# A scan and an MLP in one kernel: the MLP's first product as one run per group of half-height matmuls, with loads on two queues and a new order

## The chip, the cores and the metric

The kernel runs on one core of one Trainium2 chip. The metric is the device time of one execution in microseconds (us). Differences of about 0.2% are what a measurement of this kernel can tell apart. The core has five engines with an instruction stream each: TensorE (PE, matrix products), VectorE (DVE), ScalarE (ACT), GpSimd (POOL) and SyncE (SP, which mostly issues DMA transfers). They run beside each other and wait for each other by semaphores.

## What is computed

The input x is 2048 tokens by D = 448. It is normalised once (xn); from xn come a linear recurrence over the tokens with complex state (448 states, the "scan") and an MLP with F = 1792 hidden units and a layer norm of its own.

```python
xn = _layernorm(x)
# branch s: a diagonal recurrence over the tokens
Lam_bar = jnp.exp(dt * Lam)
Bu = jnp.einsum("bld,pd->blp", xn + 0j, ((Lam_bar - 1.0) / Lam)[:, None] * Bmat)
for t in range(L):
    h = Lam_bar[None, :] * h + Bu[:, t, :]
...
s = 2.0 * jnp.einsum("blp,dp->bld", hseq, Cmat).real + xn * Dskip
# branch g: layer norm, 448 -> 1792, gelu, 1792 -> 448, silu
y = _layernorm(xn)
g = _silu(jnp.einsum("bsf,fd->bsd", _gelu(jnp.einsum("bsd,df->bsf", y, w1) + b1), w2) + b2)
return x + s * g
```

Inputs and output are bf16.

## The kernel before, in words

**Tiling.** The 2048 tokens are 4 groups of 2 blocks of 256 tokens; in a block, even and odd tokens (`par` 0 and 1) lie apart, so that the scan takes 256 steps of two tokens per group. A group goes through these stages:

- layer norm: `ln_stats` (L356-363, DVE), `ln_scale` (L390-415), `ln_apply` (L417-429) writes the scan's input `xn_sb` and the MLP's input `xn2_sb`; `xt` (L431-446) transposes them into `xnT` and `xn2T`, by a DMA on SP, or for group 0's MLP input on PE with a copy by DVE (L446).
- `bu` (L611-624): the scan's input projection, PE at L616, 49 matmuls of 256 columns, in four parts through PSUM bank 4, each copied to `u_sb` by ACT.
- `ssm` (L629-675): the scan. DVE rotates the inputs by the tables WT into `v_sb`, does 7 scans (L641), ACT copies them to `s_b`, and DVE rotates back into `h_sb` (L669-673). Small POOL steps carry the state to the next group.
- `mm1` (L679-693): the MLP's first product. For each of the 7 pairs of F tiles, PE does 8 matmuls (L686) of 128 rows by 128 columns by 512 tokens: 2 F tiles times 4 slices of D. 448 is 3.5 times 128, so the fourth slice holds 64 rows of w1, one row with the bias b1 (against a column of ones in `xn2_sb`), and zeros. One gelu of 1024 columns (ACT, L692) takes both tiles out of PSUM; two pairs of banks take turns. For group 0 `mm1_half` (L695-709) does the same for each half of the tokens, with matmuls of 256 columns (L701), so that it can start on the first 256 tokens.
- `mm2` (L711-721): the second product, 14 matmuls of 448 columns (L715) for each of four quarters of the group, then `o` (DVE, L718), tanh (ACT, L719) and `g_sb` (DVE, L720).
- `skip` (L723-732): the term xn * Dskip for the odd tokens, on POOL or DVE.
- `ym` (L736-774): the output. 7 matmuls (L747) of `h_sb` with CZ (even tokens, with 4 more of the input with M0, L750) or CQ (odd tokens), times `g_sb` (DVE, L756), plus x (DVE, L759), and the transfer out.

Once for all groups, before that: the parameters (L455-530, mostly POOL), the tables WT (`tables`, L536-557, by ACT's Sin), the scaled and transposed B (`lb` L574, `bt`), C loaded (`ldc`, into `Cn`, L250, which is the second half of `gT`'s buffer 1) and transposed into `Cr` by DMA, CQ and CZ (`cq`, by `combine` L560-571: `tmp` on ACT or DVE at L567, then L569 on DVE), and M0 (`m0`, L599-609: four products of CQ with B, PE at L605, each of which needs all seven CQ tiles).

**What sets the order.** Every step above records tasks in a `Plan` with what they read and write. `emit` (L106-137) then goes through a list of task numbers, `ORDER` (L146-164), and gives each engine its instructions in that order; it adds a semaphore wait where a task depends on one of another engine. `SECOND` (L165-167) lists the tasks that run on their second choice of engine. An engine's stream is thus fixed: when its next instruction waits, all behind it wait. Nearly all loads are issued by SP in the order of the list.

```python
        for t in order:
...
            for sem, val in need.items():
                if seen.get(sem, 0) < val:
                    eng.wait_ge(self.sems[sem], val)
```

**PE's order before.** Group 0's first product in halves, its second products (14 + 42 matmuls, with a projection and the whole first product of group 1 in between), then M0, projections, and single pairs of group 2's first product between the other stages, so that each pair of L686 stands among scan and output work.

## Time and profile before

| | |
|---|---|
| runs | 159.75, 159.76, 159.87 us (median 159.76) |
| span of the profiled execution | 159.2 us |
| PE | 946 matmuls, 151.3 us busy (95%) |
| DVE | 265 instructions, 136.9 us (86%) |
| ACT | 151 instructions, 93.2 us (59%) |
| POOL | 51.5 us (32%) |
| TensorE clock granted | full, in all stretches but the last |
| moved by DMA | 14.70 MB, 92 GB/s on average |

The span is the profiler's, from the first to the last instruction of one execution; it is 0.56 us less than the median of the runs. "Busy" counts the time in which an engine has an instruction under way. The chain is the work that ended last, followed backwards from the end to whatever released each step. In lists of instructions a line shows the start, the length, the engine, the line of the kernel, the operation, what it writes and reads, and in brackets the idle time of the engine before it and who ended it. The groups that the steps of the first product make up are these (busy time, mean of one, then idle time of the engine before them and its cause):

```profile
L686 PE MATMUL psum<-xn2T,w_sb 128*128 128x512 bf16 x168 | 38.2, 379 | 0.1
...
L692 ACT ACTIVATE gT<-psum 128x1024 bf16<-128x1024 f32 x21 | 21.4, 1021 | 11.7 <-PE psum L686 11.6
...
L701 PE MATMUL psum<-xn2T,w_sb 128*128 128x256 bf16 x112 | 12.9, 273 | 2.0 <-DMA w_sb<-in_B_w_dram 1.8
```

Matmuls overlap in the array, so one takes 379 ns while the next follows after some 217 ns (1.73 us for eight).

### The profile page before, as it was taken

What the parts mean: (1) busy time and instruction counts of PE and PEld (TensorE: products, weight loads), DVE (VectorE), ACT (ScalarE), POOL (GpSimd) and SP (SyncE); (2) the same over time, 40 slices, a digit from 0 to 9 for tenths busy, and PEclk for the clock granted to TensorE, in tenths of its full rate; (3) what the DMA queues carried; (4) which work ended last, traced back from release to release, by engine and by line L of the source; (5) the groups of instructions that cost most, each with busy time, mean ns of one, the idle gap of its engine ahead of it and who ended that gap; (6) DMA issues with size and microseconds to landing.
All of it is one profiled execution on the core that took longest, in us unless ns stands there. A gap on an engine that the chain in (4) does not pass through costs nothing.

```text
span 159.2 us, 2725 instructions
## 1 busy us (share of the span) xinstructions
PE 151.3 (95%) x946; PEld 93.7 (59%) x946; DVE 136.9 (86%) x265; ACT 93.2 (59%) x151; POOL 51.5 (32%) x127
## 2 busy tenths in 40 slices
PE   6959999999999999999999999999989999999990
PEld 6849965565565556566655555576556655555560
DVE  5478969999998799999789999893999599999982
ACT  3839899997779962689835472212456972450200
POOL 5578840007616000038600573302015420060021
PEclk9999999999999999999999999999999999999998
DMA  4999999888980057000210430213401000010032
GB/s 103 260 303 364 315 149 198 139 161 159 276 172 4 0 100 147 0 0 4 48 20 0 120 65 1 57 21 94 116 4 58 0 4 0 0 58 0 0 115 60
DMA packets 31174, 14.70 MB, mean 92 GB/s; under 512 B 24693, under 2 KB 30713, under 8 KB 31162
## 3 DMA queue, kind: packets, MB, share of 16 engines
q1 hardware_dynamic: 30914, 14.26, 39.4%
q0 software_dynamic: 96, 0.23, 0.4%
q8 instruction: 7, 0.11, 0.3%
q10 hardware_dynamic: 152, 0.05, 0.1%
q14 instruction: 5, 0.04, 0.1%
HBM read 6.89 MB, written 1.84 MB: 55 GB/s over the span
## 4 chain that ended last, share of the span: by engine, by line
PE 88%; DMA 7%; SPq 2%; DVE 1%; issue 0%
PE psum L715 27%; PE psum L686 21%; PE psum L616 13%; PE psum L747 12%; PE psum L701 7%; PE psum L750 4%; DMA w_sb<-in_B_w_dram 4%; PE psum L605 3%; DMA xnT<-xn_sb 3%; SPq L84 2%; PE psum L753 1%; PE psum L440 0%; DVE t L756 0%; DVE tmp L759 0%; PE psum L607 0%
## 5 line engine op out<-in xcount | busy, mean ns | idle before, releaser
L715 PE MATMUL psum<-w_sb,gT 128*128 128x448 bf16 x224 | 43.8, 352 | 0.0
L686 PE MATMUL psum<-xn2T,w_sb 128*128 128x512 bf16 x168 | 38.2, 379 | 0.1
L715 PEld LDWEIGHTS psum<-w_sb,gT 128*128 128x128 bf16 x224 | 21.9, 98 | 20.0
L692 ACT ACTIVATE gT<-psum 128x1024 bf16<-128x1024 f32 x21 | 21.4, 1021 | 11.7 <-PE psum L686 11.6
L686 PEld LDWEIGHTS psum<-xn2T,w_sb 128*128 128x128 bf16 x168 | 18.5, 112 | 15.8 <-issue 0.7
L616 PE MATMUL psum<-xnT,BT 128*128 128x256 bf16 x196 | 24.0, 273 | 0.5 <-DMA xnT<-xn_sb 0.5
L616 PEld LDWEIGHTS psum<-xnT,BT 128*128 128x128 bf16 x196 | 19.0, 98 | 5.8 <-DMA xnT<-xn_sb 1.0
L719 ACT ACTIVATE th<-o 128x448 f32<-128x448 f32 x16 | 9.1, 573 | 16.4 <-DVE o L718 16.3
L641 DVE TENSOR_TENSOR_SCAN s_f<-cw,cur,v_sb 128x256 f32<-128x256 f32 x21 | 15.6, 784 | 0.2
L701 PE MATMUL psum<-xn2T,w_sb 128*128 128x256 bf16 x112 | 12.9, 273 | 2.0 <-DMA w_sb<-in_B_w_dram 1.8
L701 PEld LDWEIGHTS psum<-xn2T,w_sb 128*128 128x128 bf16 x112 | 11.8, 112 | 2.8 <-DMA w_sb<-in_B_w_dram 2.0
L620 ACT ACTIVATE u_sb<-psum 128x512 bf16<-128x512 f32 x12 | 7.2, 596 | 10.2 <-PE psum L616 10.0
L731 POOL TENSOR_TENSOR xd<-xn_sb,dbc 128x448 bf16<-128x448 bf16 x4 | 4.8, 1198 | 24.9 <-DVE dbc L339 13.9
L747 PE MATMUL psum<-CZ,h_sb 128*128 128x448 bf16 x56 | 11.9, 352 | 0.0
L756 DVE TENSOR_TENSOR t<-psum,g_sb 128x448 bf16<-128x448 f32 (+2 forms) x17 | 9.9, 589 | 1.7 <-PE psum L750 1.1
L358 DVE BATCH_NORM_STATS2 lnst<-x_all 128x6 f32<-128x448 bf16 x14 | 8.2, 611 | 3.5 <-DMA x_all<-in_A_x_dram 3.5
L720 DVE SCALAR_TENSOR_TENSOR g_sb<-th,o 128x448 bf16<-128x448 f32 x16 | 10.4, 664 | 0.7 <-ACT th L719 0.6
L718 DVE TENSOR_TENSOR o<-psum,b2bc 128x448 f32<-128x448 f32 x16 | 9.7, 614 | 1.3 <-PE psum L715 1.3
L747 PE MATMUL psum<-CQ,h_sb 128*128 128x448 bf16 (+2 forms) x54 | 10.5, 332 | 0.0
L731 POOL TENSOR_TENSOR xr<-xd,g_sb 128x448 f32<-128x448 bf16 x5 | 5.5, 1106 | 14.6 <-DVE tmp L759 14.5
L707 ACT ACTIVATE gT<-psum 128x512 bf16<-128x512 f32 x14 | 8.3, 590 | 3.2 <-PE psum L701 2.9
L731 POOL TENSOR_TENSOR xr<-x_all,xr 128x448 f32<-128x448 bf16 x6 | 6.9, 1156 | 9.2 <-DVE xr L732 9.1
(157 smaller groups left out, 224.8 us busy)
## 6 DMA issues: line engine op xcount, KB each, us to landing
out_dram<-tmp SPq DMA_DIRECT2D x7, 224.0 KB, 2.0
w_sb<-in_B_w_dram SPq DMA_DIRECT2D x3, 448.0 KB, 7.0
x_all<-in_A_x_dram SPq DMA_DIRECT2D x3, 448.0 KB, 4.4
w_sb<-in_B_w_dram SPq DMA_DIRECT2D x3, 384.0 KB, 6.2
gT<-in_A_C_re_dram SPq DMA_DIRECT2D x1, 392.0 KB, 11.6
Bn<-in_A_B_re_dram SPq DMA_DIRECT2D x1, 336.0 KB, 6.5
Bn<-in_A_B_im_dram SPq DMA_DIRECT2D x1, 336.0 KB, 6.4
gT<-in_A_C_im_dram SPq DMA_DIRECT2D x1, 336.0 KB, 12.0
```

Of the source, the lines that this page charges most:

```text
L616: fns = [lambda e, r=r, m=m, d=d: e.matmul(psum[:, 4, r * NK:(r + 1) * NK], BT[:, m, d, :], xnT[:, gx, d, :], start=(d == 0), stop=(d == 6 ...
L641: dve(lambda e, i=i, ri=ri, init=init: e.tensor_tensor_scan(s_f[:, i, ri, :], col(R2, i).to_broadcast([128, NK]), v_sb[:, i, ri, :], init, ...
L686: fns = [lambda e, k=k, d=d: e.matmul(psum[:, b0 + k, :], w1_sb[:, d, fcol(2 * j + k)], rhs[:, d, :, :], start=(d == 0), stop=(d == 3)) fo ...
L692: act(lambda e: e.activation(gT[:, gb, 2 * j:2 * j + 2, :], psum[:, b0:b0 + 2, :], ACT.Gelu_apprx_tanh), [f"ps{b0}", f"ps{b0 + 1}"] + (WK ...
L701: fns = [lambda e, k=k, d=d: e.matmul(psum[:, banks[k], :].rearrange("p (r c) -> p r c", r=2)[:, :, cs], w1_sb[:, d, fcol(2 * j + k)], rhs ...
L715: fns = [lambda e, fi=fi: e.matmul(psum[:, bk, 0:D], gT[:, gb, fi, q * 128:(q + 1) * 128], w2_sb[:, fi, :], start=(fi == 0), stop=(fi == N ...
L718: dve(lambda e: e.tensor_tensor(o2[:, fb, :], psum[:, bk, 0:D], b2bc[:], ALU.add), [f"ps{bk}", "b2bc"], [f"oo{fb}"], 0.62, prio - 76)
L719: act(lambda e: e.activation(th[:, fb, :], o2[:, fb, :], ACT.Tanh, scale=0.5), [f"oo{fb}"] + (WK + WKP if g == 0 else []), [f"th{fb}"], 0. ...
L720: dve(lambda e: e.scalar_tensor_tensor(out=g_sb[:, gs, :], in0=th[:, fb, :], scalar=1.0, in1=o2[:, fb, :], op0=ALU.add, op1=ALU.mult), [f" ...
L731: kb.either(("pool", lambda e, o=o, i0=i0, i1=i1, op=op: e.tensor_tensor(o, i0, i1, op), 1.37, 0.15), ("dve", lambda e, o=o, i0=i0, i1=i1, ...
L747: fns = [lambda e, k=k: e.matmul(psum[:, bk, c0:c1], h_sb[:, hb, k, k0:k0 + 128], cm[:, k, c0:c1], start=(k == 0), stop=False) for k in ra ...
L756: dve(lambda e: e.tensor_tensor(t3[:, fb, c0:c1], psum[:, bk, c0:c1], g_sb[:, gs, c0:c1], ALU.mult), [f"ps{bk}", f"g{gs}"], [f"t3{fb}_{c0} ...
```

## The change

- `mm1` and `mm1_half` become `mm1_run`. It does a whole group (or a token half of group 0) in one run. Each matmul uses 64 rows of the array instead of 128: the upper and lower half of the rows work on different F tiles of a pair. In phase one, F tile 0 takes its upper 64 rows of three slices and F tile 1 its lower 64; in phase two they swap, with a fourth matmul each for the half slice. So a pair is 6 + 8 = 14 half-height matmuls. Pair j + 1's phase one is issued before pair j's phase two.
- There are three pairs of PSUM banks for it (four in group 0's run), `MB`. The bias is no longer a row of w1 but an operand of the gelu (`b1f`); a pair has two gelus of 512 (or 256) columns for one of 1024 (or 512).
- The 64 last rows of w1 are loaded into rows 64 to 127 of slice 3, and 64 rows of slice 2 are copied to rows 0 to 63 of slice 3 (`w1c`, 4 copies, two on DVE and two on ACT). `xn2_sb` repeats 64 columns to match (`tcols`), so `ln_apply` for the MLP is two instructions for groups 1 to 3. The memsets of the padding go.
- C is staged in the scan's tiles `vs` (`v_sb` and `s_b` together) instead of in `gT`.
- Loads may be issued by ACT instead of SP; some are.
- Group 0's layer norm scales are worked out for both blocks together on DVE; group 1's chain of small steps moves to POOL. `skip` is split in two parts.
- `ORDER` and `SECOND` are new. The stages are recorded in the order of `STEPS`. PE's order after: group 0's run in halves; three of its second products; pairs of group 1's run (whole), with projections of group 0 and the fourth second product towards its end; then the first M0 product, with projections and second products between the four of them; group 2's run; two second products; the first output; one pair of group 3's run; the other outputs of groups 0 and 1, with group 2's projections and other second products between them; the rest of group 3's run, and then its remaining stages.

Instructions: PE 946 to 1156, DVE 265 to 260, ACT 156 to 195, POOL 129 to 138, as the programs list them.

```diff
-            def mm1(g, j, prio):
...
-            def mm1_half(j, b, k3, prio):
...
+            MB = ((0, 1), (2, 3), (4, 7), (5, 6))
+
+            def mm1_run(g, b, n0, prio):
+
+                gx = gb = g % 2
+                cols = slice(0, 256) if b is None else slice(b * 128, (b + 1) * 128)
+                rhs = xn2T[:, gx, :, cols].rearrange("p (r d) c -> p d r c", r=2)
...
+                def phase(j, second):
+
+                    c = chunk[2 * j]
+                    bk = MB[j % 3 if g else (n0 + j) % 4]
+
+                    def one(k, n, h):
+                        rows, d = slice(64 * h, 64 * h + 64), (0, 1, 2 + h, 3 - h)[n]
+                        return lambda e: e.matmul(view(bk[k]), w1_sb[rows, d, fcol(2 * j + k)], rhs[rows, d, :, :], start=not second and n == 0, stop=second and n == 3)
+                    pe([one(h if not second else 1 - h, n, h) for n in range(4 if second else 3) for h in (0, 1)],
+                       xk2 + [f"w1_{c}", f"w1r_{c}"] + ([f"w1c_{c}"] if second else []), [f"ps{bk[0]}", f"ps{bk[1]}"], prio=prio)
+                    if second:
+                        act([lambda e, k=k: e.activation(gT[:, gb, 2 * j + k, :].rearrange("p (r c) -> p r c", r=2)[:, :, cols], view(bk[k]), ACT.Gelu_apprx_tanh,
+                                                         bias=b1f[:, 2 * j + k:2 * j + k + 1]) for k in range(2)],
...
+                for j in range(8):
+                    if j < 7:
+                        phase(j, False)
+                    if j:
+                        phase(j - 1, True)
...
-                ld("sp", w1_sb[0:64, 3, a:a + w], dram_ap(B_w1, 384 * F + a, [[F, 64], [1, w]]), [f"w1r_{c}"], 64 * w * 2, prio)
+                ld("sp", w1_sb[64:128, 3, a:a + w], dram_ap(B_w1, 384 * F + a, [[F, 64], [1, w]]), [f"w1r_{c}"], 64 * w * 2, prio)
+                low, high = w1_sb[0:64, 3, a:a + w], w1_sb[64:128, 2, a:a + w]
+                kb.either(("dve", lambda e: e.tensor_copy(low, high)), ("act", lambda e: e.activation(low, high, ACT.Copy)), [f"w1_{c}"], [f"w1c_{c}"])
...
-        Cn = gT[:, 1, 6:14, :].rearrange("p (t h) c -> p t (h c)", h=2)
+        Cn = vs[:].rearrange("p (t h) r c -> p t (h r c)", h=2)
...
+                parts = [(dst, src)] if not which or not g else [(dst[:, 0:384], src[:, 0:384]), (xn2_sb[:, b, par * 512 + 384:par * 512 + 512], src[:, 320:D])]
...
+X0 L1 N1 W0 R1 W1 Z0 B00 B01 M0 M1 B02 M2 B03 M3 X1 L2 B10 B11 B12 B13 R2 Y000 Y001 Y010 Y011 N2 W2 Z1 X2 L3
+Y100 Y101 Y110 Y111 N3 Z2 X3 B20 B21 B22 B23 R3 W3 B30 B31 B32 B33 Y200 Y201 Y210 Y211 Z3 Y300 Y301 Y310 Y311
```

## The prediction, made before the result was known

> **What bounds the kernel now.** The page's busy times come first, then its chain.
>
> ```profile
> PE 151.3 (95%) x946; PEld 93.7 (59%) x946; DVE 136.9 (86%) x265; ACT 93.2 (59%) x151; POOL 51.5 (32%) x127
> ...
> PE 88%; DMA 7%; SPq 2%; DVE 1%; issue 0%
> ```
>
> TensorE (PE) is busy for 151.3 of 159.2 us and carries 88% of the chain, so a saved matmul pitch is saved time, as long as nobody else is late. VectorE (DVE) is second at 86%, so I ask where it is already full. In the stretches of 10 us (columns: PE, PEld, DVE, ACT, POOL, then clock, DMA share, GB/s):
>
> ```profile
> 30.00:40.00 10.00, 9.88 (x55) 5.54 (x54) 9.79 (x17) 8.73 (x13) 3.37 (x4) 1.00 0.82 157
> 40.00:50.00 10.00, 10.00 (x57) 5.67 (x56) 9.42 (x19) 7.63 (x11) 4.93 (x6) 1.00 0.77 172
> ...
> 60.00:70.00 10.00, 10.00 (x65) 6.25 (x63) 9.76 (x19) 5.74 (x10) 0.07 (x1) 1.00 0.27 52
> ```
>
> DVE is full from 30 to 70 us, and PE still never waits for it: its order puts work that DVE does not feed in front of it. The chain's pieces in order of time (start, length) show how PE's order goes:
>
> ```profile
> 14.33 7.09 PE psum L701 x64
> 21.42 10.59 PE psum L715 x56
> ...
> 33.66 12.26 PE psum L686 x56
> ...
> 55.39 1.32 PE psum L605 x7
> ...
> 63.71 1.73 PE psum L686 x8
> ...
> 69.40 1.64 PE psum L616 x14
> ...
> 72.76 1.53 PE psum L616 x14
> ...
> 81.00 1.32 PE psum L747 x7
> ```
>
> The DVE rows that release those two products, and the copy that starts DVE's stretch:
>
> ```profile
> 14.36 0.69 DVE L446 COPY xn2T<-psum 128x1024 bf16<-128x1024 bf16 x1 [0.39 <-PE psum L440]
> ...
> 53.86 0.68 DVE L569 SCALAR_TENSOR_TENSOR CQ<-Cr,cw,tmp 128x448 bf16<-128x448 bf16 x1
> ...
> 78.72 0.29 DVE L673 TENSOR_TENSOR h_sb<-pa 128x256 bf16<-128x256 bf16 x1
> ```
>
> The first M0 product (L605) needs all seven CQ tiles; the last ends at 54.54, and L605 starts at 55.39. The first output product (L747) needs h; that ends at 79.01, and L747 starts at 81.00. So DVE has 0.9 and 2.0 us to spare at the two places where PE needs it.
>
> **The half-height products.** A pair of F tiles costs PE eight 512-wide matmuls, 1.73/8 = 0.217 us each. The change makes 14 matmuls of 64 rows out of them. If the upper and lower halves run side by side, a pair costs 7 pitches. Groups 1 to 3: 21 pairs x 7 x 0.217 = 31.9 for 36.3 us, -4.4. Group 0: 7.09/64 = 0.111; 14 x 7 x 0.111 = 10.9 for 12.4, -1.5. No row of the trace shows two row halves. Bounds: side by side, 7 pitches; one after the other, 14. The nearest row is the two matmuls into different column halves (L458): both are 187 ns long and start within 3 ns of each other, and weight loads of 4 rows follow at (0.16 - 0.092)/3 = 0.023 us. I take 7. Two loads of 128 columns per 0.217 us are less than PE does now at 0.109 per matmul with one load each (L616), so the loads fit.
>
> Entering and leaving a tile shape: the 64-column M0 product takes 1.44 where others take 1.33, and the projection behind it 1.64 against 1.53: 0.11 each way. The new order runs the halves in 8 blocks, so 16 x 0.11 = 1.8 us, of which 10 (1.1 us) lie on the dense path behind the start. Bounds 0 and 0.16 each (latency 379 less pitch 217 ns).
>
> The Trainium skill, "TensorEngine Tiling (Array Packing)", Key Properties, speaks against the change: switching the tiling mode drains TensorE. The row above is such a price; a full drain of 0.16 would make 2.6 of 1.8. "TensorE: Matmul & The Clock Gate", Measured speedup vs the span model, gives 3.07 times for four row tiles; as an estimate, two at the same share give 1.53 where 14/8 = 1.75 is needed, and the first product would lose about 6.9 us. No run here shows either yet.
>
> **The start.** The halved group 0 loses its gain. It still waits for the first w1 piece (landing now at 10.15), and phase two waits for a copy of 64 weight rows on ACT (no row for it; between the 0.38 of a 256-wide ACT instruction and the 0.60 of a 512-wide one). The second token half needs layer norm, transposes and the copy of L446, which I put at 15.6 for 15.05, since two weight copies (0.25 to 0.45 each) go ahead on DVE. Two evacuations of 256 per pair cost ACT 2 x 0.38 = 0.76 against PE's 0.78. I let this run end at 21.5, for 21.4 now.
>
> **PE alone.** From there: second products 16 x 2.65 = 42.4; first products 31.9; projections 196 x 0.109 = 21.4; M0 5.5; outputs 27.3: 128.5; switches 1.1; small issue gaps 0.7: PE ends at 151.8. The tail stays (155.4 to 159.2, 3.75): 155.5.
>
> **ACT, POOL, SP.** ACT gets two 512-wide gelus of 0.59 for one 1024-wide of 1.02: 21 x 0.16 = +3.4, in all about +5.9 with copies, so 99 us of 160. Inside a run it needs 14 x 0.59 + moves, up to 13.6 us against PE's 10.6; a ring of three bank pairs, and work that PE has behind, hide that. The first full run follows the Sin tables: PE may stall there by up to 1.9 (between 0 and that; I count it inside the next wait). SP issues as many transfers as before, several on ACT's queue now; its transposes (1.2 to 1.7 of queue each) keep their order, and the one the first full run needs lands near 30 us, a wait of at most 0.9. C staged in scan tiles frees gT's second half: that is what lets group 1's product go ahead. The bias as an operand of the gelu, the memsets that go and the split of the skip products cost nothing on the path: POOL is busy 32%, and DVE's first 10 us 54%. What ACT gets in loads at the start it pays at SP's rate of 0.4 to 0.56 per issue in the chain, beside 4.2 us of idle time in its first 10.
>
> **DVE, the cover that fails.** PE now does group 0's four second products, 10.6, a whole run of group 1, 10.6, and three projections, 4.6, and with 0.6 of switches stands before the first M0 product at 21.5 + 26.4 = 47.9, where it was 55.4. What DVE must do for it is nearly the same. Between L446 and the last CQ, by pitches of the rows: before 34.2 us (wall 39.5, thus 5.3 of idling and of rows stretched while POOL ran, such as L424's pair of 2.03 us at 36.26). After: less a chain of ten small lnw steps 2.0, three o 1.6, two g 1.1, two xd 0.7, one CZ 0.6; more six Bn scalings 6 x 0.46 = 2.8, one of Cr 0.5, one statistic 0.7, split xn2 pieces 0.7, De and reciprocal 0.6: 33.5. From 15.6, with 0 to 5.3 added, the last CQ is done at 49.1 to 54.4; I take 4.0, nearer to the row: 53.1, a wait of 5.2 us (bounds 1.2 and 6.5).
>
> At the first output product: before 57.0 of DVE work (wall 64.0, 7.0 over). After: group 1's scan now stands ahead of the last CZ: seven scans 7 x 0.60 = 4.2 and its products and sums 6.7; Bn scalings 2.8; Cr 1.4; De and reciprocal 0.6; less lnw 2.0, g 1.6, o 1.1, xd 0.7, the rest 0.5: 66.8. From 15.6, with 0 to 7.0 added, 82.4 to 89.4; with 4.4 it is 86.8. PE comes there at 81.3 alone (70.5 of work behind it), at 86.5 after the M0 wait: 0.3 more. The outputs of group 3 wait again for their h: about 1.3 (bounds 0 and 2.0, the slack at the first output above).
>
> **Sum.** 155.5 + 5.2 + 0.3 + 1.3 = 162.3 of span. The profiled run's span is 159.2 where the runs' median is 159.76, 0.56 around it: 162.8 us.
>
> **Rivals.** (1) DVE keeps up. PE's waits on DVE must stay under 159.2 - 155.5 = 3.7 us in all; that is the point from which it is faster. For it: DVE's work alone allows 82.4 at the first output, 1 us behind PE, and idle gaps close when PE is ahead. Against it: 7.0 us over the work in the profile. Time 155.5 + 0.56 = 156.1, up to 159. (2) The waits just eat the gain: 159.4 to 160.1. (3) Halves run side by side only in part, or loads hold them (0.25 to 0.30 a pair instead of 0.217): 147 x 0.033 to 0.083 = +4.9 to +12; partly in place of the DVE waits, 166 to 172. (4) No concurrency, the change doesn't do what it says: +31.9 + 10.9 less the waits hidden, about 195.
>
> **Chances.** Forecast (DVE late) 0.46; DVE keeps up 0.30; no change 0.06; partly side by side 0.12; not at all 0.06. About 0.2% is what a measurement can tell from no change. So faster 0.30, same 0.06, slower 0.46 + 0.12 + 0.06 = 0.64. The range goes from just below PE alone, 155.8, to 168.0 in case (3); the likeliest case's own range is 160.2 to 165.
>
> **What would show it.** Right: two half-height matmuls per 0.217 us; PE waits on DVE's CQ before the first M0 product near 48 to 53 us, and on CZ or h before the first output at 84 to 88; DVE lines in the chain. Wrong: M0 without a wait, or the first output before 83 us; a pair pitch above 0.23; a PE wait on ACT's gelu of more than 2 us.

## The result, and the profile after

| | before | after |
|---|---|---|
| runs, us | 159.75 to 159.87, median 159.78 | 165.28, 165.29, 166.26, 167.60, median 165.77 |
| ratio | | 1.039, 95% interval 1.033 to 1.045 |
| profiled execution | span 159.2 | 165.28, span 163.6 |

The kernel is 6.0 us slower, where 3.0 were forecast. The busy times of the page after; its chain breaks off after a few steps, so it leads nowhere:

```profile
PE 149.8 (92%) x1156; PEld 90.3 (55%) x1156; DVE 131.8 (81%) x260; ACT 99.7 (61%) x187; POOL 63.6 (39%) x136
...
DVE 2%; issue 1%
```

PE is busy for less time (149.8 for 151.3) in a longer span. So the time went into waits. The stretches of 10 us say where (columns as before):

```profile
30.00:40.00 10.00, 8.34 (x76) 4.54 (x76) 9.17 (x17) 9.67 (x17) 5.45 (x11) 1.00 1.15 221
40.00:50.00 10.00, 9.37 (x74) 5.50 (x71) 9.93 (x23) 7.45 (x13) 5.41 (x9) 1.00 0.87 165
...
80.00:90.00 10.00, 8.48 (x49) 4.09 (x49) 7.16 (x15) 9.47 (x17) 1.94 (x6) 1.00 0.28 54
```

Before, the last of these stretches was:

```profile
80.00:90.00 10.00, 10.00 (x56) 5.36 (x55) 9.19 (x14) 4.19 (x6) 0.81 (x3) 1.00 0.13 25
```

PE was full before in each of the three, but for 0.1 us from 30 to 40. Now it lacks 1.7 us from 30 to 40, 0.6 from 40 to 50 and 1.5 from 80 to 90. From 30 to 40 ACT is at 9.67 and DMA at 1.15 (0.82 before). PE's waits in the whole run, with what released them (sum, times, longest):

```profile
PE psum L766 <- POOL cwk L670: 1.5, 1, 1.5
PE psum L469 <- DMA vrows<-in_A_log_dt_dram: 1.5, 1, 1.5
PE psum L714 <- ACT gT L718: 1.4, 1, 1.4
PE psum L802 <- POOL mhalf L305: 1.4, 1, 1.4
PE psum L629 <- DMA BT<-Bn: 0.6, 1, 0.6
PE psum L733 <- issue: 0.6, 1, 0.6
PE psum L766 <- DVE t L775: 0.5, 2, 0.2
```

No releaser stands out: POOL, ACT, DMA and DVE each hold PE once. In PE's order (start, length, and the wait in brackets) they stand here:

```profile
14.79 6.72 PE L714 MATMUL psum<-xn2T,w_sb 64*128 64x256 bf16 x120
21.45 5.47 PE L733 MATMUL psum<-w_sb,gT 128*128 128x448 bf16 x28
...
35.85 4.72 PE L714 MATMUL psum<-xn2T,w_sb 64*128 64x512 bf16 x42 [1.43 <-ACT gT L718]
...
51.67 1.48 PE L618 MATMUL psum<-CQ,Bn 128*128 128x448 bf16 x7 [0.38 <-issue]
...
68.90 11.04 PE L714 MATMUL psum<-xn2T,w_sb 64*128 64x512 bf16 x98
79.87 5.47 PE L733 MATMUL psum<-w_sb,gT 128*128 128x448 bf16 x28
...
86.86 1.49 PE L766 MATMUL psum<-CZ,h_sb 128*128 128x448 bf16 x7 [1.52 <-POOL cwk L670]
```

Read three things. The start ends at 21.45. Group 2's whole run lasts from 68.90 to 79.87: 49 pitches in 10.97 us, 0.224 each with the switches, so the two halves do run side by side (in the trace the two matmuls of a pair start 3 to 4 ns apart). The first M0 product waits only 0.38, since PE comes to it at 51.3, already late; the first output waits 1.52. "POOL cwk" there is the inferred releaser: POOL's state copy, which follows the same `h` of DVE, stands last. At the first M0 product the last CQ tile had ended 0.1 us before, at 51.56, and had itself waited for ACT's scaling:

```profile
50.71 0.85 DVE L582 SCALAR_TENSOR_TENSOR CQ<-Cr,cw,tmp 128x448 bf16<-128x448 bf16 x1 [0.43 <-ACT tmp L579]
```

**Where 4.4 us of span come from.** PE's time from the end of the start to its last matmul, split by the starts of successive groups, the waits taken out:

| PE from 21.4 us to its end | before | after |
|---|---|---|
| first product, groups 1 to 3 | 36.5 | 33.3 |
| second products | 42.2 | 43.2 |
| all else | 54.8 | 55.3 |
| work | 133.5 | 131.8 |
| waits | 0.5 | 5.4 |
| from PE's end to the end of the span | 3.8 | 5.0 |
| sum | 137.8 | 142.2 |

The mode gives 3.3 in its own product, of which some 1.5 come back in the steps around it; the new order adds 4.9 of waits and 1.2 of tail.

**Two times of the same kernel.** In every later execution of either kernel 1.7 to 1.9 us lie around the span, also in this one of after (165.28 for 163.6). So the profiled execution of before, span 159.2, would be one of about 160.95, some 1.2 above its median, and not one of 159.76 as the section on the time before has it. The rest of the 6.0 is this 1.2 and the 0.5 by which the profiled execution of after lies under its own median. The 0.2% named at the top is too fine as well: later executions of before went from 158.6 to 161.4, but for one of 162.8, and the intervals of the ratios reach 0.25 to 0.6% to either side. The profiles of e_param, d_cz, l_light and h_run below are of executions at the long end of their times; I read from them who waits for whom, not the total.

### The profile page after: what moved, and what is told of

It is laid out like the page before. It is cut to its first block, busy times and chain, and to the rows that moved or that the text cites. A ratio compares the mean times of both kernels' runs of the same rounds, so it can differ in the third digit from the quotient of the medians.

```text
span 163.6 us, 3165 instructions
## 1 busy us (share of the span) xinstructions
PE 149.8 (92%) x1156; PEld 90.3 (55%) x1156; DVE 131.8 (81%) x260; ACT 99.7 (61%) x187; POOL 63.6 (39%) x136
## 3 DMA queue, kind: packets, MB, share of 16 engines
q10 hardware_dynamic: 1984, 1.53, 3.5%
## 5 line engine op out<-in xcount | busy, mean ns | idle before, releaser
L714 PE MATMUL psum<-xn2T,w_sb 64*128 64x512 bf16 (+1 forms) x490 | 46.1, 341 | 2.2 <-ACT gT L718 1.4
L718 ACT ACTIVATE gT<-psum,b1f 128x512 bf16<-128x512 f32 (+1 forms) x70 | 37.0, 602 | 4.5 <-PE psum L714 4.3
L714 PEld LDWEIGHTS psum<-xn2T,w_sb 64*128 64x128 bf16 x490 | 27.5, 110 | 19.4 <-issue 3.9
L750 POOL TENSOR_TENSOR xr<-xd,g_sb 128x448 f32<-128x448 bf16 x7 | 7.7, 1106 | 40.3 <-DVE g_sb L738 24.7
L439 ACT ACTIVATE xn_sb<-x_all,lnw 128x448 bf16<-128x448 bf16 (+2 forms) x21 | 13.1, 664 | 8.7 <-POOL xd L750 8.2
L654 DVE TENSOR_TENSOR_SCAN s_f<-cw,cur,vs 128x256 f32<-128x256 f32 x21 | 14.9, 741 | 0.3
L658 ACT ACTIVATE vs<-s_f 128x1536 bf16<-128x1536 f32 x4 | 5.9, 1487 | 8.6 <-DVE s_f L654 8.6
L438 DVE TENSOR_SCALAR xn_sb<-x_all,lnw 128x448 bf16<-128x448 bf16 (+2 forms) x21 | 7.1, 389 | 4.6 <-ACT xn_sb L439 2.6
L750 POOL TENSOR_TENSOR xd<-xn_sb,dbc 128x448 bf16<-128x448 bf16 x7 | 9.0, 1294 | 1.5 <-DVE dbc L352 1.4
L766 PEld LDWEIGHTS psum<-CZ,h_sb 128*128 128x128 bf16 x56 | 5.4, 98 | 6.4 <-ACT gT L718 1.9
```

The source lines that it names most:

```text
L439: ("act", [lambda e, o=o, i=i: e.activation(o, i, ACT.Identity, bias=nb, scale=rs) for o, i in parts], 0.75, 0.2)]
L654: dve(lambda e, i=i, ri=ri, init=init: e.tensor_tensor_scan(s_f[:, i, ri, :], col(R2, i).to_broadcast([128, NK]), v_sb[:, i, ri, :], init, ...
L714: return lambda e: e.matmul(view(bk[k]), w1_sb[rows, d, fcol(2 * j + k)], rhs[rows, d, :, :], start=not second and n == 0, stop=second and ...
L718: act([lambda e, k=k: e.activation(gT[:, gb, 2 * j + k, :].rearrange("p (r c) -> p r c", r=2)[:, :, cols], view(bk[k]), ACT.Gelu_apprx_tan ...
L750: kb.either(("pool", lambda e, o=o, i0=i0, i1=i1, op=op: e.tensor_tensor(o, i0, i1, op), 1.37, 0.15), ("dve", lambda e, o=o, i0=i0, i1=i1, ...
L766: fns = [lambda e, k=k: e.matmul(psum[:, bk, c0:c1], h_sb[:, hb, k, k0:k0 + 128], cm[:, k, c0:c1], start=(k == 0), stop=False) for k in ra ...
```

## The experiments

All were timed beside before, whose medians were 159.72 to 160.38; each ratio is against before in the same rounds. Where only `ORDER` or `SECOND` changed, the edit is given in words, by engine. The theories at first: the mode saves, and waits of the new order eat it; the half-height mode itself costs; DVE is late; the queues and transfers are late; PE's order is wrong. In the expectations theories have letters, and each expectation says what its letters stand for.

**The mode out, the order kept (a_full).** Every pair is eight full-height matmuls again.

```diff
-                    pe([one(h if not second else 1 - h, n, h) for n in range(4 if second else 3) for h in (0, 1)],
+                    pe([one(int(second), d) for d in range(4)],
```

> The changed kernel with eight full-height matmuls per pair in place of 14 half-height ones, in the same places, order and banks (the 64 rows of w1 that stand in two slices are counted twice). Theory W (the halves do save a pitch in eight; the loss is waits behind DVE, ACT and POOL at the places where the new order makes PE ask early, and a longer tail): TensorE gets 21 x 0.217 + 14 x 0.111 = 6.1 us of work more and 1.8 of shape switches less, and about 1.5 to 3 of that fills waits: 166.5 to 169. Rival H (half-height matmuls cost more than they save, by switches and weight loads): not above 165.8. Rival Q (late parameters and a second load queue delay the start, all else is dense): 165.8 + 4.3 = 170.

167.60 us, ratio 1.050 (1.046 to 1.053): slower than after by 1.8. So in this order the mode is no cost, and the rival that blames it falls. In its profile PE's longest wait, and the clock (last column but two) in the four microseconds behind it:

```profile
PE psum L713 <- DMA xn2T<-xn_sb: 2.5, 1, 2.5
```

```profile
34.00:36.00 2.00, 2.00 (x8) 0.81 (x6) 1.30 (x3) 0.00 (x0) 1.84 (x6) 0.61 1.21 244
36.00:38.00 2.00, 2.00 (x7) 0.69 (x6) 1.45 (x3) 0.18 (x1) 0.00 (x0) 0.53 1.48 119
```

PE had waited 2.5 us for group 1's transposed input, and then worked at 0.61 and 0.53 of its clock: 2 x 0.39 + 2 x 0.47 = 1.7 us lost on top. PE's work here was 136.3, 4.5 over after; without the 1.7 the mode is worth 2.8 of PE's time in this order.

**The mode alone, the order kept from before (b_half).** Half-height for all groups, in before's list, the two phases of a pair directly behind each other.

```diff
-                fns = [lambda e, k=k, d=d: e.matmul(psum[:, b0 + k, :], w1_sb[:, d, fcol(2 * j + k)], ...
+                for fns in halves((b0, b0 + 1), j, view, rhs):
+                    pe(fns, [f"xmT{gx}_{b}" for b in range(2)] + [f"w1_{c}", f"w1r_{c}"],
```

> The kernel before, in its own order with its own two pairs of banks, with only the first product made half-height (the last 128 rows of w1 loaded as a fourth slice, bias in the gelu, two gelus per pair; phase two of a pair right behind its phase one, with a wait of PE for itself between them). Theory W: a pair that stands alone pays two switches (0.22) and a drain between its phases (0.16) for a pitch of 0.217 saved, so 14 lone pairs lose about 0.17 each, the run of seven in group 1 gains 0.5, group 0's halves lose about 0.7: 161 to 163.5; the mode pays in runs only. Rival H: 165 or more. Rival Q, by which the halves were worth their 5.9 us if the supply is as before: 155 to 158.

167.22, ratio 1.047 (1.043 to 1.050): 3.7 us above my own range, and in that of the rival by which the mode itself costs. PE hardly waits (its order is dense), but its work is 136.9. Group 1's run:

```profile
36.66 12.82 PE L693 MATMUL psum<-xn2T,w_sb 64*128 64x512 bf16 x98
```

A pair takes 1.82 there, 1.73 at full height. Seven pitches are 1.52; the other 0.30 is the wait by which the program keeps phase two behind phase one, since both write into the same banks from different rows (PE's weight loads stand there for the matmuls of phase one, seven times in this run, 3.8 us in all). A pair that stands alone among other work took 1.89 from start to next. The start, too, ended at 24.43 for 21.42: PE waited 1.28 us behind the bias's loads, which stood on ACT's queue, and a pair of its short matmuls took 1.03 for 0.89. So here the mode costs where the phases of a pair follow each other directly, and saves (1.57 for 1.73 a pair) with another pair's phase in between. That needs a run of pairs, and for the pairs that stand alone in before's list the new order is what makes the runs.

**One supply at a time.** The next six each aim at one suspect.

e_param: the sine chain of the parameters starts earlier (ACT's Abs ahead of gelus), the load of b2 goes behind it.

```diff
-ACT: gelus of group 0, Abs, gelus
+ACT: Abs, gelus of group 0
-POOL: wrap behind the layer norm, b2 load ahead
+POOL: wrap ahead, b2 load behind the sine
```

> The changed kernel with POOL's parameter chain freed: the Abs step on ACT goes ahead of the third pair's gelus (it stood behind seven pairs, at 15.6 us, where it was at 8.1 before), the wrap steps on POOL go ahead of iota and signs, and the load of b2 on POOL behind the sine steps. Parameters then come some 4 to 5 us earlier. Theory W: DVE starts the B scalings earlier, the 1.8 us that it idled for the layer norm scale go, but PE still waits 1.4 for ACT's gelu behind the Sin tables, so 0 to 1.2 us gained: 164.5 to 165.8. Rival Q: the late parameters are the cause, 2.5 to 4 us gained: 161.8 to 163.3. Rival H: no difference.

167.13, ratio 1.040 (1.034 to 1.045): no gain. The sine chain began at 12.3 for 15.9, but the late b2 made DVE wait, and group 1's run waited 2.8 for xn2T. The edit moved two things, so it says only that the chain alone does not set the time.

d_cz: DVE does the CZ tiles ahead of group 1's scan, the state copy comes behind the outputs.

```diff
-DVE: scan of group 1, last CZ tiles
+DVE: CZ tiles, scan of group 1
-POOL: state copy, outputs of group 0
+POOL: outputs of group 0, state copy
```

> The changed kernel with the first output freed: the last three CZ tiles stand ahead of group 1's scan on DVE, and POOL's copy of group 1's last state is recorded behind group 0's outputs, so that these no longer wait for it. Theory W: the 1.5 us that PE waits before the first output go, later parts move up with it except where DVE is full at the end (140 to 160 us): 0.5 to 1.5 gained, 164.3 to 165.3. Rival Q: no more than 0.5 gained. Rival H: no difference at the end, since the wait would be taken over by the next.

169.00, ratio 1.055 (1.051 to 1.060). The edit made a wait of its own: ACT's scaling for a CZ tile stood ahead of the copy of M0 and waited for DVE.

```profile
PE psum L716 <- DMA xn2T<-xn_sb: 4.8, 1, 4.8
PE psum L716 <- ACT M L622: 2.5, 1, 2.5
```

d_copy: of d_cz only the state copy.

```diff
-POOL: state copy, outputs of group 0
+POOL: outputs of group 0, state copy
```

> The changed kernel with one dependency taken off: POOL's copy of group 1's last state is recorded behind group 0's outputs, so that the first output waits for CZ and group 0's own scan only. In the profile the last CZ ends at 85.9 us and the output starts at 86.9. Theory D: at most 0.9 gained, 164.9 to 165.8, since DVE's last CZ stands behind group 1's scan anyway. Theory L: nothing that the spread would show. An order in which POOL is the bound: 1.5 gained.

166.68, ratio 1.042 (1.038 to 1.046). The first output no longer names POOL; it waits 1.6 for an ACT gelu. The copy was the last of several, not the cause.

l_light: B is scaled in one column only. I expected that to take some 8 us off DVE; in the profile it is 5.4 (126.4 us busy for 131.8).

```diff
+                w = 1 if wr[:2] == "LB" else D
+                o, a, b = o[:, 0:w], a[:, 0:w], b[:, 0:w]
```

> The changed kernel with DVE relieved: the scaling of B is done on one column of 448 only (eight products and seven sums, some 8 us of DVE; the rest of that half of B is zeros), everything else in place and in order. Theory D: the CQ tiles and the last CZ come up to 8 us earlier, PE's waits before the first M0 product and the first output go, the tail behind the end does not: 161.5 to 164. Theory L: the wait for group 1's input stays, 164.5 to 165.8. Rival H (PE's own half-height work is the loss): no difference, 165.5 to 166.

166.48, ratio 1.038 (1.033 to 1.044): as after. DVE now idles 5.7 us for x, and PE waits elsewhere:

```profile
PE psum L718 <- DMA xn2T<-xn_sb: 4.6, 1, 4.6
```

That speaks against the theory that I forecast with: DVE has 5.4 us less to do, the first M0 product no longer waits, and nothing is won. The last CQ tile came no earlier either (55.00): in this execution it waited 1.61 for ACT's scaling.

f_xsp: the last two blocks of x are loaded by SP, not by ACT, whose stream had stood 2.27 us at that issue behind a transpose of C (gelus behind it).

```diff
-SECOND: ... 214 ...   (load of x, blocks 6 and 7, issued by ACT)
+SECOND: ... ...
```

> The changed kernel with one load moved: x of the last two blocks is issued by SP again, not by ACT. On ACT it waits for the first transpose of C, and ACT's Sin steps behind it idle 2.3 us (3.7 in the profile with the early parameters). Theory A (ACT's queue is what holds group 1's first product): the 1.4 us that PE waits for the gelu go and stay gone: about 164.3 in the median. Theory D (DVE's supply is the bound behind it): the wait moves to the first M0 product, 0 to 0.5 gained. Theory L (in most executions PE waits 2 to 5 us for the landing of group 1's transposed input, and runs at half clock for some us after it; that and not the order of engines sets the median): no more than 0.5 gained and the spread of 165 to 169 stays.

165.16, ratio 1.034 (1.029 to 1.038), not told from after. PE's wait for the gelu is gone; the next transpose holds it instead, and the first M0 product starts at 51.38 where it started at 51.67:

```profile
41.23 1.69 PE L629 MATMUL psum<-xnT,BT 128*128 128x256 bf16 x14 [2.20 <-DMA xnT<-xn_sb]
```

g_xt: f_xsp, and SP issues group 1's transposes ahead of C's first.

```diff
-SP: transpose C, transposes xn2T of group 1
+SP: transposes xn2T of group 1, transpose C
```

> As the last one, and on SP the first transpose of C stands behind the two transposes of group 1's MLP input, not ahead of them. Theory L: the input lands 1 to 2 us earlier, the wait of PE goes in most executions, the executions draw together (all clocks above 0.99), and the median falls to 163.5 to 164.8. Theory D: C comes later, so the CQ tiles do too, and the first M0 product takes back what was gained: 165.3 to 166.3. Theory A: as for the last one.

168.16, ratio 1.049 (1.045 to 1.054), worse by 3 us than f_xsp. No wait for the input is left, though it landed no earlier (31.04 for 30.46 in f_xsp). The transposes behind it come later, and the projection's wait grows from 2.20 to 3.25; the clock falls to 0.83 and 0.50 there.

```profile
42.00:44.00 2.00, 1.14 (x8) 0.92 (x9) 2.00 (x5) 1.31 (x3) 0.00 (x0) 0.83 0.85 166
44.00:46.00 2.00, 2.00 (x10) 1.23 (x9) 2.00 (x7) 0.93 (x3) 0.00 (x0) 0.50 0.89 164
```

**Several at once.** All on top of f_xsp. q_r1: PE does the fourth second product of group 0 ahead of group 1's run.

```diff
-PE: 3 second products, run of group 1, ..., 4th
+PE: 4 second products, run of group 1
```

> The changed kernel with x of the last blocks issued by SP, and the fourth second product of group 0 (2.65 us of PE work that is ready at 29.4 us) put ahead of group 1's first product, where the kernel before has it, instead of behind it. Theory C (what is lost is cover: at each place PE's next work stands on a transfer, ACT or DVE that comes just then, with nothing ready in front of it): the waits for the landing of group 1's input and for the gelu go, the executions draw together, and the wait for the scan's input behind the run (2.2 us with x on SP) goes too; the first M0 product starts at 50 to 51.5: 164.2 to 165.0. Theory S (the DMA queues are the bound until 40 us and deliver everything later than PE asks): the wait only moves behind the run, no gain against 165.2.

166.00, ratio 1.037 (1.033 to 1.041). xn2T is in time; PE then waits 2.85 at the projection (46.46), for `xn_sb`.

n_x: only 8 columns of x are loaded for the last four blocks (groups 2 and 3 take x of groups 0 and 1).

```diff
+                few = b0 > 3
+                ld(eng, x_all[:, b0, :, 0:8] if few else x_all[:, b0:b0 + n, :, :],
```

> The changed kernel with x of the last blocks issued by SP, and of those 0.9 MB only eight columns loaded (groups 2 and 3 are computed from the x of groups 0 and 1). The order now issues these loads at 29 to 33 us, before they came at 37 and 40. Theory S: with 0.9 MB less in the time in which the DMA engines are full, the input of group 1's run and of the scan land earlier; PE's waits of 2 us there go: 162.5 to 164. Theory C: PE's waits are taken over by the M0 product's wait for the last CQ (51.6): 164.5 to 165.2.

165.92, ratio 1.034 (1.031 to 1.037): some 0.9 MB less to load changes nothing.

o_first: CZ ahead of the scan on DVE (its scalings too), group 2's last three gelus ahead of group 1's copies on ACT, copy behind the outputs. k_both: o_first and q_r1.

```diff
-DVE: scan of group 1, last CZ
+DVE: last CZ, scan of group 1
-ACT: copies of group 1, last 3 gelus
+ACT: last 3 gelus, copies of group 1
```

> The changed kernel with x of the last blocks issued by SP, and the first output freed on all engines: the last CZ tiles stand ahead of group 1's scan on DVE (with their last product on DVE too), the gelus of group 2's last three pairs ahead of group 1's copies on ACT (these give back the bank that the first output needs), and POOL's state copy behind group 0's outputs. Theory C: the 1.5 us of wait before the first output go and nothing takes them over before group 3's end: 163.5 to 164.3. If group 1's scan, later by 3 us, is then late for its own outputs: 164.7 to 166.

165.11, ratio 1.030 (1.027 to 1.033): with k_both the lowest ratio of the new order, and still 3% above before. The first output starts at 84.83 without a wait (86.86 in after). The run of group 3, two products later, then waits for its own input:

```profile
84.83 1.49 PE L768 MATMUL psum<-CZ,h_sb 128*128 128x448 bf16 x7
...
88.68 2.35 PE L716 MATMUL psum<-xn2T,w_sb 64*128 64x512 bf16 x20 [1.61 <-DMA xn2T<-xn_sb]
```

> Both edits together: the second product ahead of group 1's run, and the first output freed. Theory C: the gains add: 162.5 to 164. Theory S or a bound on DVE: no more than the better one alone.

165.91, ratio 1.029 (1.025 to 1.034), the same as o_first alone: the two do not add up.

z_floor: k_both, n_x and l_light in one.

> All four lightenings of the supplies together on the changed kernel's order: only 8 columns of x of the last four blocks are loaded (groups 2 and 3 work on x of groups 0 and 1), B is scaled in one column only (the rest of the scaled B is zero), the fourth second product of group 0 stands ahead of group 1's run, CZ ahead of group 1's scan, and the state copy behind the outputs. So the computation is not the reference's in x and in B. PE's work behind the start measured 131.3 to 131.8 in four kernels, the start ends at 21.5 to 21.9, the tail is 4.95, and 1.75 lie around the span. Theory S (several supplies in series, each as late as the next; one alone freed shows the next): with all of them freed PE's waits of 5 us fall to about 1, thus 21.7 + 131.5 + 1 + 4.95 + 1.75 = 160.9, 159.5 to 162, which is still not below the kernel before. Rival R (the waits are round trips of the order itself, PE to ACT to DVE and back, whatever the supplies): 164 or more, waits of 4 us or more.

165.39, ratio 1.033 (1.029 to 1.038). The theory that freed supplies bring 160.9 missed by 4.5 us; the rival's number was met. Where the time stood, though, was a supply that I had not freed, so the run does not decide between the two. PE's wait, and SP's stream (start, length):

```profile
46.19 1.69 PE L635 MATMUL psum<-xnT,BT 128*128 128x256 bf16 x14 [3.14 <-DMA BT<-Bn]
```

```profile
34.15 3.40 SPq L83 DMA_TRANSPOSE BT<-Bn  x2
37.59 1.30 SPq L83 DMA_TRANSPOSE xnT<-xn_sb  x1
38.93 1.29 SPq L83 DMA_TRANSPOSE Cr<-vs  x1
40.27 6.67 SPq L83 DMA_TRANSPOSE BT<-Bn  x5
```

From 34 to 47 SP issues nothing but transposes, 1.2 to 2.1 us each, one behind the other, and they land some 3.1 us after their issue. PE needs the scaled B's transposes (BT) earlier in the new order, and with these issues in this order the queue does not give them; another order of them was not tried.

**The mode where a run stands anyway, in before's order.** Only group 1's seven pairs, with interleaved phases and three pairs of banks; all other pairs at full height. The 64 rows that the mode needs twice lie in the scan's tiles.

```diff
-                for j in range(7 if g else 0):
+                if g == 1:
+                    mm1_run(g, 0)
+                for j in range(7 if g > 1 else 0):
...
+            MB = ((0, 1), (2, 3), (5, 7))
```

> The kernel before, with half-height matmuls only in the one place where it has a whole run of the first product (group 1, 7 pairs), with interleaved phases and three pairs of banks; order and all else as before. Added: the last 64 rows of w1 loaded a second time, two small loads of the bias, one copy of 64 rows by 512 on DVE, and 14 gelus of 512 for 7 of 1024. Theory H (the mode is worth what its pitches say where a run stands anyway, and the new order is what costs): 7 x 7 x 0.217 + 0.22 of switches = 10.85 for 12.26, so PE gains 1.4; at the first M0 product DVE has 0.9 to spare, less 0.25 for the copy, so 0.7 to 1.4 arrive at the end: ratio 0.991 to 0.996, some 158.4 to 159.3. Rival B (PE's gain is turned into a wait for DVE, since DVE is full from 30 to 70 us): ratio 0.998 to 1.003, with a wait of about 1.4 at the first M0 product. Rival L (the loads and the gelus come late): above 1.005, with a PE wait on the bias, the copy or the gelu in the run.

160.56, ratio 1.003 (1.000 to 1.006). PE waited 2.17 for xn2T, and the four microseconds from 34 on ran at 0.68 of the clock. I put that down to the added loads, which stand ahead of the transposes on SP's queue; the trace does not show it. The second transpose of xn2T was issued earlier than before (29.45 for 30.15) and landed later (34.33 for 33.52), and PE itself came 1.3 us earlier, after a shorter start. The next version takes the loads off that queue:

```diff
-            ld("sp", w1h[64:128, 0:F], dram_ap(B_w1, 384 * F, [[F, 64], [1, F]]), ["w1h"], 229376, S1)
+            dve(lambda e: e.tensor_copy(w1h[64:128, 0:F], w1_sb[0:64, 3, :]), [f"w1r_{c}" for c in range(4)], ["w1h"])
-            ld("sp", b1c[:, 0:12] ...
+            ld("pool", b1c[:, 0:12] ...
```

> As h_run, but its added transfers are taken off the queue that carries the transposes: the bias's two small loads (3.75 us of SP's time, 9 to 11 us to land in h_run) go to POOL's queue behind the parameters, and the second copy of the last 64 rows of w1 is made by DVE (idle for 1.3 to 2 us there) instead of a load of 224 KB. In h_run's profile PE stood before group 1's run for 2.2 us, for the transposed input, and the granted clock was at 0.68 in the 4 us behind that. Theory H (the mode is worth its pitches once nothing it adds delays a transfer): the wait falls to what it was before or a little more (0 to 0.8), 1.4 are saved in the run, 0.25 + 0.5 of DVE's slack is used: 158.6 to 159.4, ratio 0.993 to 0.998. Rival B (PE gains time only to wait for the transposed input or CQ): ratio 0.999 to 1.003, with a wait of 1 us or more at group 1's run or at the first M0 product.

160.52, ratio 1.004 (1.002 to 1.007), so 0.7 us slower than before. That wait is gone, and ACT holds PE instead. PE's line, and ACT's:

```profile
37.97 1.70 PE L718 MATMUL psum<-xn2T,w_sb 64*128 64x512 bf16 x13 [1.19 <-ACT gT L723]
```

```profile
35.36 1.28 ACT L723 ACT_TABLE_LOAD   x1 [1.42 <-PE psum L718]
36.65 2.42 ACT L723 ACTIVATE gT<-psum,b1f 128x512 bf16<-128x512 f32 x4
```

ACT sat idle for 1.42 us, was released by PE, and only then loaded the gelu's table. h_run3 lets DVE do the second half of group 1's input 0.6 earlier.

```diff
-DVE: 2 pieces of xn2, sum o, 2 pieces of xn2
+DVE: 4 pieces of xn2, sum o
```

> As h_run2, and DVE makes the two last pieces of group 1's normalised input ahead of one sum with the second bias (o), so that the second transpose may start 0.6 us sooner. Theory H: as h_run2 or up to 0.5 us better, if that transpose ends PE's wait; if PE did not wait for it in h_run2, the same as h_run2, or 0.2 worse where the fourth second product waits for its bank. Rival B: as h_run2, since the landing is set by the transfers that are under way, not by the issue.

160.51, ratio 1.005 (1.003 to 1.007): no difference from h_run2, as expected for a PE that did not wait there; it stands 1.19 for the gelu again. h_run4 is h_run2 with a gelu of one column ahead of that wait.

```diff
+                act(lambda e: e.activation(warm[:, 0:1], b1f[:, 0:1], ACT.Gelu_apprx_tanh), ["b1f"] + WK, ["warmg"])
```

> As h_run2, and ACT does a gelu of one column of the bias right behind its last tanh of group 0. In h_run2's profile PE stands 1.19 us in group 1's run for pair 0's gelu: ACT had been idle for 1.42 us when that gelu was released, and only then loaded its table, 1.28 us (in the kernel before the same load lies at 34.66, while PE still has a free pair of banks). The one-column gelu brings the load into the idle time. Theory H (the mode is worth its pitches; what hides it is one late step after another): the wait of 1.19 goes and the later pairs keep their 1.51 us, so 1.2 to 1.6 under h_run2: 158.9 to 159.3, ratio to the kernel before 0.994 to 0.998. Rival B (the gain turns into the next wait, CQ at the first M0 product or the transposed input): 159.8 to 160.6 as h_run2, with a PE wait of 0.8 us or more there.

160.05, ratio 0.999 (0.996 to 1.002). The run takes 11.14 us where it took 12.10 before. As much is lost again behind the run:

```profile
44.12 1.70 PE L624 MATMUL psum<-xnT,BT 128*128 128x256 bf16 x14
46.90 8.12 PE L753 MATMUL psum<-w_sb,gT 128*128 128x448 bf16 x42 [1.08 <-ACT gT L725]
```

h_run5 moves the scaling that stood ahead of the last gelus on ACT, and one CQ tile on DVE.

```diff
-ACT: scaling for CQ3, last 4 gelus of group 1
+ACT: last 4 gelus of group 1, scaling for CQ3
-DVE: sum o, CZ1, sum o, g, CQ6
+DVE: sum o, CQ6, CZ1, sum o, g
```

> As h_run4, with the two steps moved that stood in the way of its gain: ACT does the scaling for CQ3 (which waited 0.94 for DVE) behind the last four gelus of group 1 instead of ahead of them, and DVE does CQ6 behind the first sum with the second bias instead of two such sums later. In h_run4's profile the run is 11.14 long where it was 12.10, and the next second product then stands 1.08 for those gelus; the last CQ ended 0.7 before the first M0 product. Theory H (the mode pays what it saves once the steps behind it follow): the wait of 1.08 goes, 0.7 to 1.1 under h_run4: 158.9 to 159.4, ratio to the kernel before 0.989 to 0.994. Rival B (no slack anywhere: the next wait holds it): 159.8 to 160.3, ratio 0.997 to 1.002, with a wait of 0.6 us or more at the first M0 product or at the first output.

159.61 beside 160.07, ratio 0.998 (0.994 to 1.002): the fastest version of all, by a margin that its interval does not separate from none. PE's waits, complete, and the group behind the run:

```profile
PE psum L821 <- POOL mhalf L302: 1.4, 1, 1.4
PE psum L739 <- DMA w_sb<-in_B_w_dram: 0.8, 1, 0.8
PE psum L739 <- DVE xn2T L392: 0.3, 1, 0.3
```

```profile
45.71 8.12 PE L753 MATMUL psum<-w_sb,gT 128*128 128x448 bf16 x42
53.66 1.49 PE L613 MATMUL psum<-CQ,Bn 128*128 128x448 bf16 x7
```

All that are left lie in the start; before had one more, 0.51 for xnT at 117.02. From the projection ahead of the run to its last matmul PE takes 122.3, in before 123.6 (31.85 to 155.40). So in this execution PE's end gains 1.2 us, once three steps in the way (a load, a table, a scaling) have been moved; 0.5 of that is the wait that before had, and the run itself is 0.9 shorter (11.24 for 12.10). The missing wait is what theory H expected, the ratio lies in the range of rival B; that the gain reaches the time is not shown.

## Why the prediction was wrong

The direction was right. What failed is the step "DVE, the cover that fails": it put one wait of 5.2 us before the first M0 product, where PE waited 0.38, while 2.9 us had gone before that to other waits. "The tail stays" and "0.56 around it" failed too, by 1.2 and 1.1 us. That PE's end still came within 0.1 us of the forecast is luck.

- **Half-height pairs, 7 pitches.** Right. 0.224 per pitch with the switches; first product -3.3, forecast -4.4 with 1.1 for switches. The estimate of 1.53 times for two row tiles, worked out from the 3.07 for four in the Trainium skill, "TensorE: Matmul & The Clock Gate", Measured speedup vs the span model, was too low for this case: 14 half-height matmuls in 10.97/7 = 1.57 us are 1.94 times 14 x 0.217.
- **Switches.** About right inside the run: 10.97 - 49 x 0.217 = 0.34 for entry, exit and all, forecast 0.22. But the second products and the outputs' M0 matmuls came out 1.3 longer in all (0.193 for 0.189 a pitch, 0.198 for 0.190), which I had not counted.
- **The start.** 21.45, forecast 21.5.
- **PE's end.** 158.64, forecast 158.55 (162.3 less the tail). That agrees by luck, since the parts do not (in brackets the forecast): work 131.8 (130.3), waits 5.4 (6.8). The single wait of 5.2 at the first M0 product was 0.38. PE had lost 2.9 before it: 0.60 at a second product, 0.23 for xn2T, 1.43 for a gelu, 0.63 for BT. The first output waited 1.52 (0.3), group 3's outputs 0.4 (1.3).
- **"DVE, the cover that fails."** This step failed. It put 5.2 us on DVE in one place; the 2.9 us lost before that place came in four pieces, none of them for a CQ tile, and only the gelu's 1.43 was foreseen (as up to 1.9, counted inside that wait). The last CQ tile was done at 51.56 for 53.1 and had itself waited for ACT. l_light took 5.4 us off DVE and won nothing; whichever of DVE, ACT, POOL or the transposes was relieved, the next held PE.
- **"Its transposes keep their order ... a wait of at most 0.9."** In the profiled execution of after this held: 0.23, landed at 30.42. It did not hold in those of five variants of the new order, where xn2T held group 1's run for 1.1 to 4.8 us. In two others it held group 3's run, for 1.1 and 1.6, and in five the transposes of the projection held PE for 1.2 to 3.25; above 2 us the clock mostly fell as well. I had counted SP's issues, not where each lands when the transposes stand back to back. Whether the 0.5 us between the profiled execution of after and its median come from there was not traced.
- **"The tail stays (3.75)."** This step failed: 4.96, +1.2. In the last microseconds DVE is behind PE:

```profile
157.52 1.23 DVE L778 TENSOR_TENSOR tmp<-t,x_all 128x448 bf16<-128x448 bf16 x1
157.79 0.27 PE L772 MATMUL psum<-CQ,h_sb 128*128 128x256 bf16 x1
...
158.78 0.96 DVE L775 TENSOR_TENSOR t<-psum,g_sb 128x448 bf16<-128x448 f32 x2
...
160.34 0.45 DVE L778 TENSOR_TENSOR tmp<-t,xr 128x192 bf16<-128x192 bf16 x1
```

  The product at 157.79 is taken up at 158.78, behind a sum that took 1.23, where the same sum takes 0.38 at 159.65. POOL worked beside it from 157.19 to 158.49, which may be the reason and was not tested. Before, DVE's last instruction began 0.5 behind PE's end, here 1.7.
- **"0.56 around it."** This step failed: 1.7. The span and the median came from different executions. +1.1.

Sum: span 163.6 for 162.3, of it 1.2 the tail and 0.1 PE's end; 1.1 around it; 0.5 from the profiled execution to the median: 2.9 of the 3.0.

Rival (1), DVE keeps up, allowed 3.7 us of waits on DVE. Those that DVE's rows end come to 0.6 us, with the first M0 product and the first output to 2.5 at most, so its condition held; its time, 156.1 to 159, did not come, because it left out the waits on others (5.4 in all), the tail and the time around the span. Rival (2), a gain just eaten, falls by the time. Rivals (3) and (4), halves not side by side, fall by a_full and the run of 10.97.

Open is how much of after's median over its best execution belongs to late transposes, and whether a version of the new order with B's transposes earlier, or made by PE, would reach before. Neither was tried. If PE lost no time at all behind the start, the span would be 163.6 - 5.4 = 158.2, about before's usual 158.0: so the new order could at best have tied, unless its tail were mended too.

## What to carry to other kernels

In this kernel PE is 95% busy and hardly waits, other steps arrive just in time for it, and a shorter product finds the next one late: 1.4 us on paper in one run became 0.7 to 0.8 us lost in three versions (in the first of them not told from none) and 0.3 and 0.5 us won in the last two (not told from none either), after the steps in the way had been pulled forward in turn. Before a saved pitch is counted, list for each stage which transfer, table load or copy ends last, and by how much it comes before the engine needs it; the gain is bounded by that list. And span and time belong together only if they are of the same execution.

## What the runs showed of the hardware that was not expected

- Two 64-row matmuls of different row halves run fully side by side (0.224 us per pair of 512, with the switches), but a phase that waits for the one just before it, on the same banks, paid 0.30 a pair (b_half).
- A short stop of PE can have a second price. Waits of 2.17 to 4.8 us were followed by some 4 us at 0.57 to 0.69 of the clock on average (a_full, d_cz, g_xt, e_param, l_light, h_run; k_both a little later). In after itself the clock was 0.50 and 0.70 from 8 to 10 and 10 to 12 us, 2 us behind a stop of 1.48 for `vrows`; the start ended no later for it (21.45; 21.30 in e_param, without it). Six variants did the same after stops of 1.2 to 2.1 there, six others kept the clock after stops of 1.2 to 1.8, and so did f_xsp (2.20), q_r1 (2.85) and z_floor (3.14) at their long waits. So the length of a stop alone does not decide it here. The Trainium skill, "TensorE: Matmul & The Clock Gate", HAM oscillation, has the same picture of stops that re-throttle the clock; it names about 3.4 us, and here 1.5 was enough in one execution and 3.1 not in another.
- Two loads for the bias in pieces of 8 and 4 bytes, 3.5 KB together, kept SP's queue for 3.75 us in h_run and landed after 9 to 11 us. The loads of C issued just ahead of them took 12, so the small pieces are not shown to be the reason for the landing; like pieces landed in 3.3 to 3.7 in after.
